# Moving the division, cutting GpSimd's splits in four, and reordering the first loads in a fused attention and expert kernel

## The chip, the core and the metric

One core of a Trainium2 chip. TensorE (PE) multiplies, VectorE (DVE) and ScalarE (ACT) do elementwise work and reductions, GpSimd (POOL) does elementwise work and issues the indirect transfers, SyncE (SP) issues the other transfers. Each engine takes its instructions in the order in which the program was written; engines wait for each other by semaphores. The metric is device time of one execution in microseconds (us).

## The reference

```python
# attention, for 4 batches x 8 heads, 768 positions, 64 dims
k_sum = k.reshape(B, H, 24, 32, D).max(axis=3)
v_sum = v.reshape(B, H, 24, 32, D).mean(axis=3)
scores_l = scale * q @ k.T, kept where |i - j| < 16
scores_s = scale * q @ k_sum.T + log(32)
a = softmax(concat(scores_l, scores_s))
x = a @ concat(v, v_sum)                    # then (4, 768, 512)
# a token's expert: argmax of 8 logits, or the expert of the token before it
fresh_e = argmax(x @ w_gate);  local = sigmoid(x @ w_local)
e = fresh_e if s == 0 or local < 0.5 else previous e
out = softmax(logits)[e] * (relu(x @ w1[e]) @ w2[e])   # 512 -> 1024 -> 512
```

All is float32. The products of the experts are made of three matmuls on split operands: each operand is a high part (the value rounded to the format fp32r) and a low part (the rest), and hi x hi, hi x lo and lo x hi are added.

## The kernel before

**Attention.** A pair is two heads of one batch; there are 16 pairs, and each is worked in two groups of three blocks of 128 queries, 32 groups G in all. A group passes through stages that are issued in different rounds of one loop over G: its scores (`s_mm`, L251 mask and L257), its maximum on DVE (L264) and exponentials on ACT (L268), two rounds later its transposes on PE (L278) with copies on ACT (L279), three rounds later the second products (`a_mm`, L289) into a PSUM pool `a` of one bank, and the division `a_norm` on DVE (L300, L302, L304), which reads that bank. Before the change `a_norm` of a group stands one round after its `a_mm`, between the transposes and the maximum of that round, and two calls `small(1)` stand between its three instructions.

**Keys and values of a pair.** `load_k`, `load_q`, `load_v`, `load_w` fetch keys (two buffers), queries (three), values for the sums (two) and values for the windows (`vw`, three) through SP's queue. POOL copies the keys into overlapping windows (`windows`, L216), halves the values for their sums (`fold_v`, L209), writes the summary columns (`summaries`, L219) and spreads the value sums into `vw` (`spread_v`, L228). DVE reduces keys (L200) and values (`reduce_v`, L204); `sum_v` transposes the sums on PE (L223) and copies them on ACT. In an even round 2n POOL gets `windows(n + 1)` and `fold_v(n + 1)`, in the odd one `summaries(n + 1)` and `spread_v(n)`. A transfer into a buffer that is still to be read waits in SP's queue, and so do all transfers behind it.

**Routing.** When a batch's x is done, `x_tile` makes its logits on PE, and `route`, `early`, `second`, `gate_p`, `finish` work out each token's expert and place, in many small DVE instructions with PE steps between them. They are generators that yield the kind of the next step. Inside the attention `small(n, pe)` issues up to n of them at fixed places, from at most two chains in turn; a step LONG counts 4; a PE step is taken only where `pe` is set and at least `AGE` = 2 calls after the step before it. A round has five calls before the change (1, 1, 3, then 2 and 4 with PE), 11 in sum. After the attention `flow` places them by a plan of time: a DVE step counts `C_DVE` and its result `C_LAT` more, a PE step is issued when the plan's time has reached its operand. The first rows of tokens for the experts' fourth pair of slots are listed by matmuls at L852, the weights of the rows by L938; `self.A` holds a one-hot row of 128 for each token (L581), which L700, L727, L852 and L938 use.

**Experts.** Rows come in slots of 128, two to a pair. The first three pairs hold the most frequent experts and run while `route` and `finish` still work on the last batch. A pair is 96 matmuls of the first layer (L1015 to L1017), ReLU (L1021 ACT, L1023 DVE), and 24 of the second for each half (L988 to L990). Rows are fetched (L960) and written (L1001) by indirect transfers from POOL. A new expert's weights are split in eight chunks of 1024 columns by `split`: ACT rounds (L951), DVE or POOL subtracts (L954), by a letter for each chunk (`WBY`, `SPLIT_BY`).

Of the kernel before, what the change touches and what calls it, by code (L numbers as in the profile page):

```python
# [9 lines left out]
F32 = mybir.dt.float32  # L10
# [3 lines left out]
AF = mybir.ActivationFunctionType  # L14
ALU = mybir.AluOpType
# [4 lines left out]
P = 128  # L20
# [36 lines left out]
AGE = 2  # L57
C_T, C_PE, C_WAIT, C_LONG, C_DVE, C_LAT, AHEAD = 0.65, 0.8, 0.3, 0.9, 0.17, 0.05, 1.5

# [3 lines left out]
class Kernel:  # L63
    def __init__(self, ctx, tc, qT, kT, vT, vW, maskc, identc, wgc, w1, w2, c32c, cb16c, out):
        self.tc, self.nc, self.out = tc, tc.nc, out
        self.steps, self.credit, self.have_p, self.last, self.early_in = [], 0, 0, None, {}
        self.calls = 0
        self.t, self.q = 0.0, 0.0
        self.qT, self.kT, self.vT, self.vW = qT, kT, vT, vW
        self.w = (w1, w2)  # L70
# [73 lines left out]
    def attention(self, tick, last):  # L144
        nc, tc, ident = self.nc, self.tc, self.ident
        with ExitStack() as ctx:
# [44 lines left out]
            nc.sync.dma_start(out=t, in_=src)  # L191
            for load, n in ((load_k, 1), (load_q, 1), (load_v, 0), (load_w, 0), (load_v, 1), (load_w, 1), (load_q, 2)):
                load(n)
# [18 lines left out]
            def windows(n, eng=nc.gpsimd, t0=0, t1=NW):  # L212

                src = kp[n % 2][:, 64 * t0:64 * t0 + 1]
                win = bass.AP(src.tensor, src.offset, [src.ap[0], (64, t1 - t0), (1, WL)])
                eng.tensor_scalar(out=kb[n % 2][:, t0:t1, 0:WL], in0=win, scalar1=0.125, scalar2=1.0, op0=ALU.mult, op1=ALU.mult)  # L216

# [74 lines left out]
            def a_norm(G):  # L292
                n, g = groups[G]
                b, p = pairs[n]
                ap = live.pop(G)
                if p == 0:
                    self.xs[b, g] = wk.tile([P, NG, H * D], F32, name="xs", bufs=4)
                x = self.xs[b, g]
                dn = wk.tile([P, NG, 2, 1], F32, name="dn")
                nc.vector.tensor_scalar(out=dn, in0=ap[:, :, :, D:D + 1], scalar1=1e-9, scalar2=None, op0=ALU.add)  # L300
                self.small(1)
                nc.vector.reciprocal(out=dn, in_=dn)  # L302
                self.small(1)
                nc.vector.tensor_tensor(  # L304
                    out=x[:, :, 2 * D * p:2 * D * (p + 1)].rearrange("p u (h d) -> p u h d", h=2),
                    in0=ap[:, :, :, 0:D], in1=dn.to_broadcast([P, NG, 2, D]), op=ALU.mult)
                if p == NP - 1:
                    t = b * NU + NG * g
                    nc.sync.dma_start(out=self.x_dram[:, t:t + NG, :], in_=x)

            reduce_k(0)
            windows(0, nc.vector, 0, NW // 2)
            windows(0, nc.gpsimd, NW // 2, NW)
            summaries(0, nc.vector)
            windows(1)
            load_k(2)
            LT, LA = 2, 3
            last_g = len(groups)
            for G in range(last_g + LA):
# [7 lines left out]
                tick(G, 2)  # L327
                if G < last_g and G % GP == 0 and G:
                    sum_v(G // GP, self.spare[:, 1, 0:P])
                tick(G, 4)  # L330
                if LT <= G < last_g + LT:
                    t_stage(G - LT)
                if LA + 1 <= G <= last_g:
                    a_norm(G - LA - 1)
                tick(G, 3)
                if G < last_g:
                    s_exp(G)
                    self.small(3)
                if G == 0:
# [3 lines left out]
                if G < last_g:  # L343
                    self.small(2, True)
                if LA <= G:
                    a_mm(G - LA)
                if G < last_g:
                    n, g = groups[G]
# [14 lines left out]
                    else:  # L363
                        if n == 0:
                            sum_v(0, self.bank("t")[:, 0:P])
                            reduce_v(1)
                        elif n + 1 < N:
                            summaries(n + 1)
                            reduce_v(n + 1, folded.pop(n + 1))
                        spread_v(n)  # L370
                        if n + 3 < N:
                            load_k(n + 3)
                            load_q(n + 3)
                else:
                    a_norm(G - LA)
                tick(G, 1)
# [12 lines left out]
    def wait(self):  # L389
        while len(self.steps) > 1:  # L390
            yield "WAIT"

# [91 lines left out]
    def route(self, b):  # L484
# [55 lines left out]
        yield "DVE"  # L540
        v.tensor_tensor_scan(out=s2, data0=c["keep"], data1=o2, initial=0.0, op0=ALU.mult, op1=ALU.add)
        yield "PE"
        m = self.bank("t")
# [29 lines left out]
        if b == 1:  # L573
# [3 lines left out]
                                   op0=ALU.mult, op1=ALU.max)  # L577
        for u in range(NU):
            if u % 2 == 0:
                yield "DVE"  # L580
            v.tensor_scalar(out=self.A[:, b * NU + u, :], in0=c["iota128"], scalar1=lanf[:, u:u + 1],  # L581
                            scalar2=None, op0=ALU.is_equal)

# [20 lines left out]
    def second(self):  # L604
# [14 lines left out]
        yield "DVE"  # L619
        v.scalar_tensor_tensor(out=cnt, in0=self.er, scalar=2.0 * P, in1=cnt, op0=ALU.mult, op1=ALU.max)  # L620
        yield "DVE"
        v.tensor_tensor(out=self.lbe[:, 0:1], in0=e1f, in1=self.e0f, op=ALU.is_equal)
# [14 lines left out]
        yield "DVE"  # L637
        v.tensor_scalar(out=self.adj[:, 2], in0=self.is1, scalar1=-2.0, scalar2=7.0, op0=ALU.mult, op1=ALU.add)

    def gate_p(self, b0, b1):  # L640
# [30 lines left out]
        for i in range(3):  # L671
            yield "DVE"
            v.tensor_copy(out=p3[:, :, i, 0], in_=r)
            if i < 2:
                yield "DVE"
                v.tensor_tensor(out=r, in0=r, in1=p3[:, :, i, 0], op=ALU.subtract)

    def early(self, j, ef=None, places=None):

        nc, wk, c = self.nc, self.rw, self.c  # L680
        v = nc.vector
        n = self.early_b(j) * NU
        ef, places = ef or self.e0f, places or (2.0 * j, 2.0 * j + 1)
        in0 = self.early_in[j] = wk.tile([P, n, 2, 1], BF16, name=f"ein{j}")
# [19 lines left out]
        for i in range(2):  # L704
            yield "DVE"
            v.scalar_tensor_tensor(out=self.lb[:, 0:n], in0=in0[:, :, i], scalar=64.0, in1=self.lb[:, 0:n], op0=ALU.mult, op1=ALU.add)

    def early_b(self, j):
# [3 lines left out]
    def early_p(self, b0, b1, *pairs):  # L712
        nc, wk, v = self.nc, self.rw, self.nc.vector
        yield from self.gate_p(b0, b1)
        for j in pairs:
            while j not in self.early_in:
                yield "WAIT"
            in0 = self.early_in[j]
            n = self.early_b(j) * NU
# [31 lines left out]
    def finish(self):  # L751
# [4 lines left out]
        npi = wk.tile([P, E], I32, name="npi")  # L756
        nci = wk.tile([P, E], I32, name="nci")
        q = wk.tile([P, E], F32, name="q")
        yield "DVE"
# [164 lines left out]
        yield from rows(FIRST, SLOTS)  # L924
        yield from self.gate_p(B - 1, B)
        n = SLOTS - EARLY
        eq = wk.tile([P, NT, n], F32, name="eqp")
# [21 lines left out]
    def split(self, which, c0, c1, src, eng):  # L949
        hi, lo = self.hi[which][:, c0:c1], self.lo[which][:, c0:c1]  # L950
        self.nc.scalar.copy(out=hi, in_=src)  # L951
        if eng is self.nc.vector:
            self.dve(1.1)
        eng.tensor_tensor(out=lo, in0=src, in1=hi.bitcast(F32), op=ALU.subtract)  # L954

# [388 lines left out]
```

## Time and profile before

| | us |
|---|---|
| times of three runs | 493.34, 495.4, 497.38 (median 495.4) |
| the profiled execution | 497.38 |
| its span, first to last instruction | 495.6 |
| PE busy | 448.0 (90% of the span) |
| DVE, ACT, POOL busy | 285.2, 216.4, 190.1 |
| mean granted clock of PE | 0.957 |

A row of the order of time gives start, length, engine, line, operation, what is written from what, the shape and the count; in brackets the idle time before it and the instruction that ended it. A row of groups gives busy time, mean length in ns, and idle time with its releasers. A `q` behind an engine's name is its sequencer, where transfers are issued.

### The profile page before, as it was taken

Reading aid. Unit: us, or ns where it says so; the run is one execution under the profiler, and the core shown is the slowest. Engines: PE = TensorE matmul, PEld = TensorE weight load, DVE = VectorE, ACT = ScalarE, POOL = GpSimd, SP = SyncE. Lnnn points to the kernel's source line nnn. Section 1 sums busy time; section 2 is a strip of 40 time slices with the busy share of each in tenths; the row PEclk is TensorE's granted clock in tenths of the full one; section 3 lists DMA queues with packets and bytes.
Section 4 is the critical chain, followed back from the end, with each engine's and each line's share of the span. In section 5 each row is a group of like instructions: output and inputs, shape, how many; then the busy total and the mean of one; then the engine's idle time right before and its main releaser. Section 6 shows DMA issues by size and latency. Waiting matters only on the chain. (4 is left out here: it accounts for less than half of the span.)

```text
span 495.6 us, 11918 instructions
## 1 busy us (share of the span) xinstructions
PE 448.0 (90%) x4400; PEld 389.0 (78%) x4400; DVE 285.2 (58%) x623; ACT 216.4 (44%) x478; POOL 190.1 (38%) x152
## 2 busy tenths in 40 slices
PE   6899988878779999889899999999999999999990
PEld 5687776767567789688799998989879898977980
DVE  4686698777663756965522223158686226777610
ACT  3698876677535322702110201054556116274500
POOL 2685553373401230631102111146477204566720
PEclk9799999979879999979999999999999999999996
DMA  8999799678212084016402010119498503847840
GB/s 317 404 370 375 285 321 395 239 256 341 88 56 75 1 296 173 21 65 231 197 1 85 23 65 28 58 43 323 145 324 280 197 33 110 309 165 253 291 162 26
DMA packets 23622, 92.04 MB, mean 186 GB/s; under 512 B 2927, under 2 KB 3567, under 8 KB 19440
## 3 DMA queue, kind: packets, MB, share of 16 engines
q1 hardware_dynamic: 18752, 76.11, 42.2%
q0 software_dynamic: 4640, 14.68, 8.7%
q8 instruction: 41, 0.67, 0.5%
q14 instruction: 45, 0.37, 0.2%
q10 hardware_dynamic: 144, 0.20, 0.1%
HBM read 78.40 MB, written 13.11 MB: 185 GB/s over the span
## 5 line engine op out<-in xcount | busy, mean ns | idle before, releaser
L1015 PE MATMUL bs<-xT,h 128*128 128x256 f32 x384 | 110.6, 288 | 0.0
L1016 PE MATMUL bs<-xT,h 128*128 128x256 f32 x384 | 109.5, 285 | 0.5 <-DVE xT L966 0.5
L1017 PE MATMUL bs<-xT,l 128*128 128x256 f32 x384 | 109.6, 285 | 0.1
L1021 ACT ACTIVATE hT<-bs 128x512 fp32r<-128x512 f32 x48 | 28.7, 598 | 131.8 <-PE bs L1017 127.7
L960 POOL DMA_INDIRECT xg<-x_dram,gidx x32 | 34.8, 1089 | 127.5 <-POOLq L1191 57.7
L988 PE MATMUL ba<-h,hT 128*128 128x512 f32 x192 | 77.7, 405 | 0.4
L1023 DVE SCALAR_TENSOR_TENSOR hT<-bs,hT 128x512 fp32r<-128x512 f32 x48 | 33.0, 690 | 77.7 <-ACT hT L1021 66.8
L1016 PEld LDWEIGHTS bs<-xT,h 128*128 128x128 f32 x384 | 74.5, 194 | 1.1 <-DVE xT L966 0.7
L990 PE MATMUL ba<-h,hT 128*128 128x512 f32 x192 | 75.1, 391 | 0.0
L989 PE MATMUL ba<-l,hT 128*128 128x512 f32 x192 | 75.0, 391 | 0.0
L1015 PEld LDWEIGHTS bs<-xT,h 128*128 128x128 f32 x384 | 74.5, 194 | 0.7 <-issue 0.2
L1017 PEld LDWEIGHTS bs<-xT,l 128*128 128x128 f32 x384 | 74.4, 194 | 0.5 <-DVE l L954 0.5
L954 DVE TENSOR_TENSOR l<-stg,h 128x1024 fp32r<-128x1024 f32 x35 | 67.9, 1949 | 11.3 <-ACT h L951 8.1
L268 ACT ACTIVATE pr<-bs,nm 128x120 f32<-128x120 f32 x192 | 52.0, 372 | 25.2 <-DVE nm L264 24.8
L951 ACT CAST h<-stg 128x1024 fp32r<-128x1024 f32 x56 | 57.2, 1052 | 11.3 <-PE ba L990 8.2
L954 POOL TENSOR_TENSOR l<-stg,h 128x1024 fp32r<-128x1024 f32 x21 | 51.4, 2467 | 20.4 <-ACT h L951 20.4
L1001 POOL DMA_INDIRECT out_dram<-yo,sidx x26 | 31.1, 1197 | 59.1 <-DVE yo L1000 40.2
L988 PEld LDWEIGHTS ba<-h,hT 128*128 128x128 f32 x192 | 36.1, 188 | 8.0 <-ACTq L1191 0.6
L289 PE MATMUL ba<-vw,pt 120*64 120x65 f32 x768 | 33.0, 241 | 10.3 <-DVE xs L304 5.9
L990 PEld LDWEIGHTS ba<-h,hT 128*128 128x128 f32 x192 | 36.0, 188 | 7.8
L289 PEld LDWEIGHTS ba<-vw,pt 120*64 120x64 f32 x768 | 28.9, 153 | 15.7 <-issue 11.6
L989 PEld LDWEIGHTS ba<-l,hT 128*128 128x128 f32 x192 | 36.2, 189 | 6.2
(236 smaller groups left out, 672.3 us busy)
## 6 DMA issues: line engine op xcount, KB each, us to landing
stg<-in_w SPq DMA_DIRECT2D x32, 1024.0 KB, 5.7
vw<-in_vW SPq DMA_DIRECT2D x16, 780.0 KB, 4.5
kp<-in_kT SPq DMA_DIRECT2D x16, 384.0 KB, 6.3
q<-in_qT SPq DMA_DIRECT2D x16, 384.0 KB, 6.7
vt<-in_vT SPq DMA_DIRECT2D x16, 384.0 KB, 7.3
x_dram<-xs SPq DMA_DIRECT2D x8, 768.0 KB, 9.9
wst<-in_w SPq DMA_DIRECT2D x8, 512.0 KB, 8.4
xg<-x_dram,gidx POOLq DMA_INDIRECT x32, 8.4
```

The costliest lines, as they stand in the source:

```text
L268: nc.scalar.activation(out=pr[:, h, u, :], in_=sp[:, h, u, :], func=AF.Exp, bias=nm[:, h, u:u + 1], scale=1.0)
L289: nc.tensor.matmul(out=ap[64 * c:64 * c + 64, u, h, :], lhsT=pt[:, h, u, 64 * c:64 * c + 64], rhs=vw[n % 3][0:W, 2 * (NG * g + u) + c, h, ...
L951: self.nc.scalar.copy(out=hi, in_=src)
L954: eng.tensor_tensor(out=lo, in0=src, in1=hi.bitcast(F32), op=ALU.subtract)
L960: self.nc.gpsimd.indirect_dma_start(out=t, out_offset=None, in_=rows, in_offset=bass.IndirectOffsetOnAxis(ap=self.gidx[:, i:i + 1], axis=0))
L988: nc.tensor.matmul(out=ps, lhsT=ah, rhs=wh, start=first, stop=False)
L989: nc.tensor.matmul(out=ps, lhsT=ah, rhs=wl, start=False, stop=False)
L990: nc.tensor.matmul(out=ps, lhsT=al, rhs=wh, start=False, stop=last)
L1015: nc.tensor.matmul(out=ps[:, j], lhsT=wh, rhs=xh, start=(k == 0), stop=False)
L1016: nc.tensor.matmul(out=ps[:, j], lhsT=wh, rhs=xl, start=False, stop=False)
L1017: nc.tensor.matmul(out=ps[:, j], lhsT=wl, rhs=xh, start=False, stop=(k == KT - 1))
L1023: nc.vector.scalar_tensor_tensor(out=l, in0=ps, scalar=0.0, in1=h.bitcast(F32), op0=ALU.max, op1=ALU.subtract)
```

## The change

- `a_norm(G - 3)` is issued right behind `a_mm(G - 3)`, without the two `small(1)`. A round has three calls of `small` (3, 2, 4), 9 in sum, and PE steps are allowed in all of them.
- `reduce_v(n + 1)` moves ahead of `a_mm` in odd rounds.
- `sum_v` and `spread_v` of pairs 0 and 1 move behind the transposes of rounds 2 and 4; `reduce_v(1)` moves from round 1 to round 3.
- The first loads: values 0 ahead of queries 1; values 1, `vw` 1 and queries 2 behind keys 2. Half of the first `windows` is done by ACT instead of DVE.
- `split`: where POOL subtracts, four instructions of 256 columns stand for one of 1024.
- `route`: the six one-hot rows L581 become one `tensor_tensor` for all, a LONG step.
- `until(names)` lets a chain yield WAIT until another has reached a named point (`done`); it issues nothing.
- `C_DVE` is 0.1 for 0.17.

```diff
-C_T, C_PE, C_WAIT, C_LONG, C_DVE, C_LAT, AHEAD = 0.65, 0.8, 0.3, 0.9, 0.17, 0.05, 1.5
+C_T, C_PE, C_WAIT, C_LONG, C_DVE, C_LAT, AHEAD = 0.65, 0.8, 0.3, 0.9, 0.1, 0.05, 1.5
...
-            for load, n in ((load_k, 1), (load_q, 1), (load_v, 0), (load_w, 0), (load_v, 1), (load_w, 1), (load_q, 2)):
+            for load, n in ((load_k, 1), (load_v, 0), (load_q, 1), (load_w, 0)):
                 load(n)
...
-                eng.tensor_scalar(out=kb[n % 2][:, t0:t1, 0:WL], in0=win, scalar1=0.125, scalar2=1.0, op0=ALU.mult, op1=ALU.mult)
+                if eng is nc.scalar:
+                    eng.activation(out=kb[n % 2][:, t0:t1, 0:WL], in_=win, func=AF.Copy, scale=0.125)
+                else:
+                    eng.tensor_scalar(out=kb[n % 2][:, t0:t1, 0:WL], in0=win, scalar1=0.125, scalar2=1.0, op0=ALU.mult, op1=ALU.mult)
...
                 nc.vector.tensor_scalar(out=dn, in0=ap[:, :, :, D:D + 1], scalar1=1e-9, scalar2=None, op0=ALU.add)
-                self.small(1)
                 nc.vector.reciprocal(out=dn, in_=dn)
-                self.small(1)
...
-            windows(0, nc.vector, 0, NW // 2)
+            windows(0, nc.scalar, 0, NW // 2)
             windows(0, nc.gpsimd, NW // 2, NW)
             summaries(0, nc.vector)
             windows(1)
-            load_k(2)
+            for load, n in ((load_k, 2), (load_q, 2), (load_v, 1), (load_w, 1)):
+                load(n)
...
-                if G < last_g and G % GP == 0 and G:
+                if GP < G < last_g and G % GP == 0:
                     sum_v(G // GP, self.spare[:, 1, 0:P])
                 tick(G, 4)
                 if LT <= G < last_g + LT:
                     t_stage(G - LT)
-                if LA + 1 <= G <= last_g:
-                    a_norm(G - LA - 1)
+                if G in (2, 4):
+                    sum_v(G // 2 - 1, self.bank("t")[:, 0:P])
+                    spread_v(G // 2 - 1)
                 tick(G, 3)
                 if G < last_g:
                     s_exp(G)
-                    self.small(3)
+                    self.small(3, True)
...
+                n, g = divmod(G, GP)
+                if g == 1 and 0 < n < len(pairs) - 1:
+                    reduce_v(n + 1, folded.pop(n + 1))
                 if LA <= G:
                     a_mm(G - LA)
+                    a_norm(G - LA)
...
-                        if n == 0:
-                            sum_v(0, self.bank("t")[:, 0:P])
+                        if n + 1 < N and n:
+                            summaries(n + 1)
+                        if n == 1:
                             reduce_v(1)
-                        elif n + 1 < N:
-                            summaries(n + 1)
-                            reduce_v(n + 1, folded.pop(n + 1))
-                        spread_v(n)
+                        if n > 1:
+                            spread_v(n)
...
+    def until(self, *names):
+
+        while not self.done.issuperset(names):
             yield "WAIT"
...
-        for u in range(NU):
-            if u % 2 == 0:
-                yield "DVE"
-            v.tensor_scalar(out=self.A[:, b * NU + u, :], in0=c["iota128"], scalar1=lanf[:, u:u + 1],
-                            scalar2=None, op0=ALU.is_equal)
+        if b < B - 2:
+            self.done.add(("counts", b + 1))
+        yield "LONG"
+        v.tensor_tensor(out=self.A[:, ts, :], in0=c["iota128"].unsqueeze(1).to_broadcast([P, NU, P]),
+                        in1=lanf.unsqueeze(2).to_broadcast([P, NU, P]), op=ALU.is_equal)
...
         if eng is self.nc.vector:
             self.dve(1.1)
-        eng.tensor_tensor(out=lo, in0=src, in1=hi.bitcast(F32), op=ALU.subtract)
+            eng.tensor_tensor(out=lo, in0=src, in1=hi.bitcast(F32), op=ALU.subtract)
+            return
+
+        for o in range(0, c1 - c0, 256):
+            p = slice(o, o + 256)
+            eng.tensor_tensor(out=lo[:, p], in0=src[:, p], in1=hi[:, p].bitcast(F32), op=ALU.subtract)
```

More of the change, by code (lines that the diff above doesn't have):

```diff
@@ L68, in __init__ @@
         self.t, self.q = 0.0, 0.0
+        self.done = {("counts", 0), ("early", -1)}
         self.qT, self.kT, self.vT, self.vW = qT, kT, vT, vW
@@ L373, in attention @@
                             load_q(n + 3)
-                else:
-                    a_norm(G - LA)
                 tick(G, 1)
@@ L390, in wait @@
         while len(self.steps) > 1:
+            yield "WAIT"
+    def until(self, *names):
+        while not self.done.issuperset(names):
             yield "WAIT"
@@ L541, in route @@
         v.tensor_tensor_scan(out=s2, data0=c["keep"], data1=o2, initial=0.0, op0=ALU.mult, op1=ALU.add)
+        yield from self.until(("counts", b))
         yield "PE"
@@ L620, in second @@
         v.scalar_tensor_tensor(out=cnt, in0=self.er, scalar=2.0 * P, in1=cnt, op0=ALU.mult, op1=ALU.max)
+        self.done.add(("counts", B - 1))
         yield "DVE"
@@ L638, in second @@
         v.tensor_scalar(out=self.adj[:, 2], in0=self.is1, scalar1=-2.0, scalar2=7.0, op0=ALU.mult, op1=ALU.add)
+        self.done.add("second")
     def gate_p(self, b0, b1):
@@ L676, in gate_p @@
                 v.tensor_tensor(out=r, in0=r, in1=p3[:, :, i, 0], op=ALU.subtract)
+        self.done.add(("weights", b0))
     def early(self, j, ef=None, places=None):
@@ L682, in early @@
         n = self.early_b(j) * NU
+        yield from self.until(("early", j - 1))
         ef, places = ef or self.e0f, places or (2.0 * j, 2.0 * j + 1)
@@ L706, in early @@
             v.scalar_tensor_tensor(out=self.lb[:, 0:n], in0=in0[:, :, i], scalar=64.0, in1=self.lb[:, 0:n], op0=ALU.mult, op1=ALU.add)
+        self.done.add(("early", j))
     def early_b(self, j):
@@ L717, in early_p @@
                 yield "WAIT"
+            yield from self.until(("weights", 0))
             in0 = self.early_in[j]
@@ L757, in finish @@
         nci = wk.tile([P, E], I32, name="nci")
+        yield from self.until("second", ("early", EARLY // 2 - 1))
         q = wk.tile([P, E], F32, name="q")
@@ L925, in finish @@
         yield from self.gate_p(B - 1, B)
+        yield from self.until(("weights", 0), ("weights", 2))
         n = SLOTS - EARLY
```

## The prediction

> **What bounds the kernel now.** I read the span first, then busy time and granted clock in stretches of 20 us, then the waits and the order of time in each stretch where TensorE (PE) is not full.
>
> ```profile
> span 495.6 us, 11918 instructions
> ```
> ```profile
> 0.00:20.00 20.00, 13.94 (x194) 11.74 (x194) 8.91 (x16) 9.06 (x29) 6.36 (x14) 0.83 0.93 349
> 20.00:40.00 20.00, 19.69 (x429) 16.36 (x425) 17.55 (x38) 18.51 (x63) 16.38 (x18) 1.00 1.01 381
> 80.00:100.00 20.00, 16.04 (x300) 12.73 (x290) 16.36 (x44) 12.52 (x43) 8.19 (x8) 0.91 0.80 299
> 100.00:120.00 20.00, 16.49 (x270) 13.77 (x272) 14.68 (x35) 14.75 (x43) 11.56 (x9) 0.83 0.81 290
> 120.00:140.00 20.00, 13.41 (x229) 10.44 (x221) 15.27 (x60) 11.15 (x36) 7.56 (x7) 0.90 0.34 117
> 200.00:220.00 20.00, 15.21 (x100) 13.45 (x99) 17.02 (x37) 9.06 (x11) 12.25 (x7) 0.83 0.15 53
> 240.00:260.00 20.00, 17.53 (x144) 16.40 (x143) 6.51 (x9) 3.67 (x6) 2.00 (x2) 1.00 0.08 31
> ```
>
> The columns are busy time of PE, its weight load, VectorE (DVE), ScalarE (ACT), GpSimd (POOL), then the granted clock, the DMA share and GB/s. PE's work sets the end, and what can be won is PE's idle time and the clock it loses. From 80 to 140 us PE is idle for 60 - 45.94 = 14.1 us, and the clock loses 0.09, 0.17 and 0.10 of 20 us, 7.2 us together. From 200 to 220 it is idle 4.8 us. In the first 20 us it is idle 6.1 us, but there the transfers are full (share 0.93, then 1.01).
>
> **The start.** The columns of the next rows are start, length, engine, line, and in brackets idle time and its releaser.
>
> ```profile
> 0.73 0.39 SPq L162 DMA_DIRECT2D kp<-in_kT  x1
> ...
> 4.83 0.95 DVE L200 TENSOR_REDUCE ks<-kp 128x24 f32<-128x768 f32 x1 [3.81 <-DMA kp<-in_kT]
> ...
> 14.16 0.39 PE L223 MATMUL bs<-ident,va 128*24 128x128 f32 x1 [2.64 <-DVE va L204]
> ...
> 16.09 0.33 SPq L167 DMA_DIRECT2D vt<-in_vT  x1
> ...
> 19.06 1.02 POOL L209 TENSOR_TENSOR vf<-vt 128x384 f32<-128x384 f32 x1 [0.72 <-DMA vt<-in_vT]
> ...
> 20.11 0.55 DVE L204 TENSOR_REDUCE va<-vf 128x24 f32<-128x384 f32 x1 [1.31 <-POOL vf L209]
> ...
> 20.53 0.62 PEld L257 LDWEIGHTS bs<-kb,q 64*64 64x64 f32 x24 [0.28 <-POOL kb L219]
> ...
> 25.73 0.35 PE L251 MATMUL bs<-me 64*64 64x360 bf16 x4
> ```
>
> The change takes the wait at 14.16 away: the sums of the first two pairs move behind the transposes of groups 2 and 4. It loads the third keys before the second values, and hands half of the first windows to ACT. But group 4's scores need `summaries(2)`, which stands on POOL behind `fold_v(2)`, and that waits for the third values. Before them lie the same bytes as now, so they land at 19 us again and group 4 starts at 20.5 again. PE is now merely idle later: from about 16 to 20.5 in one piece, with the half clock behind it where the groups follow each other closely. Two things are new. `reduce_v(2)` stands in DVE's order ahead of the division of group 0 and of `reduce_v(1)`; it ends at 20.66 (20.11 + 0.55), the division takes about 0.9 (L304 below and two small ones), `reduce_v(1)` 0.95, so the second values' buffer is free at 22.5. SyncE's load of the fourth values, issued at 16.09 now, waits for that buffer, and behind it in SP's queue wait the third `vw` and the fifth keys and queries. A load with an empty queue takes some 4 us (the first keys, asked for at 0.73, are there at 4.83), then fold 1.0 and summaries 0.4: the scores of group 6 start at 28.0 and not at 25.73. The half clock over groups 4 and 5 costs about the same, at the same time. I take **+2.3**; bounds 0 (the sums' two waits gone are enough) and +5 (a load takes its median 7.3, below).
>
> ```profile
> vt<-in_vT SPq DMA_DIRECT2D x16, 384.0 KB, 7.3
> ```
>
> **The attention groups that carry routing.** The single bank of the second products (L289) is freed by the division (L300, L302, L304). Now the division is queued a group later, with routing steps between its instructions.
>
> ```profile
> 84.21 0.56 DVE L304 TENSOR_TENSOR xs<-ba,dn 128x384 f32<-128x384 f32 x1
> ...
> 84.87 1.57 PE L289 MATMUL ba<-vw,pt 120*64 120x65 f32 x24 [2.25 <-issue]
> ```
> ```profile
> 101.09 2.35 POOL L954 TENSOR_TENSOR l<-wst,h 128x1024 fp32r<-128x1024 f32 x1 [4.59 <-ACT h L951]
> ...
> 103.41 0.44 POOL L219 TENSOR_SCALAR kb<-ks 128x288 f32<-128x288 f32 x1
> 103.90 0.85 PE L257 MATMUL bs<-kb,q 64*64 64x120 f32 x24 [1.97 <-POOL kb L219]
> ...
> 107.48 1.57 PE L289 MATMUL ba<-vw,pt 120*64 120x65 f32 x24 [1.33 <-DVE xs L304]
> ```
> ```profile
> 124.61 0.45 PE L700 MATMUL bt<-ebt,A 128*128 128x4 bf16 x12 [1.87 <-DVE ebt L696]
> ...
> 132.47 0.92 PE L289 MATMUL ba<-vw,pt 120*64 120x65 f32 x24 [1.24 <-DVE xs L304]
> ...
> 137.78 0.92 PE L289 MATMUL ba<-vw,pt 120*64 120x65 f32 x24 [2.46 <-DVE xs L304]
> ```
>
> With the division right behind its products the bank is free a whole group before it is wanted again, whatever DVE does in between. That removes 2.25 + 1.33 + 1.24 + 2.46 = 7.28 us of idle. The wait at 124.61 comes from the one-hot rows:
>
> ```profile
> L581 DVE TENSOR_SCALAR A<-c,lanf 128x128 bf16<-128x128 f32 x24 | 11.7, 543 | 0.0
> L843 DVE TENSOR_TENSOR eq<-c,blk 128x768 f32<-128x768 f32 x1 | 0.9, 934 | 0.0
> L954 POOL TENSOR_TENSOR l<-stg,h 128x1024 fp32r<-128x1024 f32 x21 | 51.4, 2467 | 20.4 <-ACT h L951 20.4
> L209 POOL TENSOR_TENSOR vf<-vt 128x384 f32<-128x384 f32 x14 | 14.2, 1011 | 8.1 <-DMA vt<-in_vT 4.5 <-DVE va L204 2.4 <-DVE cnt L553 1.2
> ```
>
> Six of 543 ns, 3.3 us, become one of the size of L843, 0.93. I count the 1.87 as gone; sum 9.2. Of the 7.2 us of clock I take half, 3.6, since the wait at 103.90 stays: it is POOL's order (`summaries` behind a weight split). There the quarters cost: two rows give (2467 - 1011) / 640 = 2.3 ns an element and so 0.72 us for 256, four of them 2.9 and not 2.47, **+0.4** once; later splits have POOL's idle time as cover (2.0 of 20 us busy from 240 on), and cost 0.4 on each of 21 chunks if it were gone. Attention: **-12.8**, bounds -5 (the bank's waits, partly replaced) and -19 (12 idle, 7.2 clock).
>
> What is late next there: DVE, with 46.3 of 60 us busy. Waiting in order for the products costs it little, because the maximum (L264) of the next group must wait for the scores that PE issues after those products. Fewer steps a group (9 for 11) and PE steps allowed at three calls in three delay the chain by less than a group. The `until` names issue nothing; they are a guard only.
>
> [...]
>
> **The end of routing.** PE stands before the matmuls that list the first rows.
>
> ```profile
> 201.13 2.04 DVE L823 TENSOR_SCALAR o<-pt 128x24 int32<-128x24 int32 x1
> ```
> ```profile
> 206.77 5.65 POOL L954 TENSOR_TENSOR l<-stg,h 128x1024 fp32r<-128x1024 f32 x2 [1.56 <-ACT h L951]
> ```
> ```profile
> 207.83 2.34 DVE L835 CAST_PREDICATED blk<-e,pt 128x24 f32<-128x24 int32 x1
> 210.20 2.33 DVE L843 TENSOR_TENSOR eq<-c,blk 128x96 f32<-128x96 f32 x1
> ```
> ```profile
> 213.09 0.80 PE L852 MATMUL bt<-bt,A 128*128 128x8 bf16 x24 [4.79 <-DVE bt L848]
> ```
> ```profile
> 218.74 0.60 ACT L1021 ACTIVATE hT<-bs 128x512 fp32r<-128x512 f32 x1 [8.76 <-PE bs L1017]
> 221.62 0.60 ACT L1021 ACTIVATE hT<-bs 128x512 fp32r<-128x512 f32 x1 [2.28 <-PE bs L1017]
> ```
> ```profile
> 236.46 0.17 DVE L659 TENSOR_SCALAR sm<-sm 128x6 f32<-128x6 f32 x1
> 236.67 0.19 DVE L661 RECIPROCAL sm<-sm 128x6 f32<-128x6 f32 x1
> ```
> ```profile
> 242.83 1.34 PE L938 MATMUL bt<-bp,A 128*128 128x108 bf16 x24 [2.47 <-DVE bp L934]
> ```
>
> Three small DVE instructions took 6.7 us together; small ones take about 0.2 (L659), so some 6.0 of it is standing until a POOL split ends. L835 ended and L843 began between the two splits of 206.77: DVE gets in at the border of two POOL instructions. With quarters a border comes every 0.72, half of it on average, 1.1 for three: DVE's chain is 4.9 shorter. Against this stands the planner: a dependent step now counts 0.10 + 0.05 and takes 0.21 (236.46 to 236.67), where it counted 0.17 + 0.05. Some 34 steps lie between the start of `finish` and L852, so PE's matmuls are placed 2.0 us too early. The wait becomes 4.79 - 4.9 + 2.0 = 1.9, a gain of 2.9. The slow clock behind it (first block of the pair from L852's end, 213.9, to 218.74, 4.8 against 2.9) cost 1.9; half goes, 1.0. The denser plan should bring L938 inside the third pair and remove its 2.47; with the same doubt I take half, 1.2. Together **-5.1**, bounds 0 and -9.2.
>
> **Sum.** The profiled execution took 497.4 us (span 495.6 and 1.8 around it), 2.0 above the median 495.4. 497.4 + 2.3 + 0.4 - 12.8 - 5.1 = 482.2; on the median **480.2**.
>
> **Rivals.**
> 1. DVE and the transfers take PE's place. For it: DVE is busy 17.55 of 20 us from 20 to 40 and 46.3 of 60 later, and the loads are full to 40. Then only about half of the 12.8 comes and half of the 5.1: 480.2 + 6.4 + 2.6 = 489.2. Against: after 80 us the transfer share is 0.8 and less.
> 2. The quarters don't let DVE in, because POOL's next one starts at once: nothing at the end of routing, 485.3. Against: the border at 210.2.
> 3. The other side: in every group the division, now ahead of the next maximum, delays the exponentials. ACT is busy 18.51 of 20 us from 20 to 40, so ACT would be the bound; price up to 0.9 (L304 0.56 and two small ones near 0.2, as L659) in 28 groups, 25 us, so 505. It decides from about 0.6 us a group. Against: the next maximum waits for the next scores anyway, and their 0.85 (L257) covers the division.
> 4. Short gaps keep the clock: removing them wins their idle time alone, 480.2 + 3.6 + 1.0 = 484.8. [...]
>
> **Chances.** Forecast 0.58, its own range 470 to 489; rival 1 0.17, rival 2 0.09, rival 3 0.10, rival 4 0.06. The range goes from 469 to 494, which leaves out rival 3 and some tails. About 1% (5 us) is what a measurement can tell from no change. Faster (under 490.4): 0.55 + 0.09 + 0.08 + 0.06 = 0.78; slower (over 500.4): rival 3's upper part, 0.08 with tails; the same: 0.14.
>
> **What would show it.** Right: no L289 that waits for L304 between 80 and 140; L257 still waiting some 2 us behind a POOL split near group 26; L823, L835 and L843 under 1 us; L852's wait between 0 and 3. At the start: the load of the fourth values after 21 us and group 6 later than 25.73. Wrong: exponentials that wait for the maximum in every group, PE waits at L512 to L938 that add up to more than 7.3, or a clock under 0.9 from 80 to 140 without long gaps.

## The result, and the profile after

The changed kernel takes 480.2 us (479.85 to 480.55) beside 496.1 for the kernel before (four runs by now), a ratio of 0.968 with a 95% interval of 0.963 to 0.974. One of its four runs took 708.2 us at a mean granted clock of 0.56; it counts in the median of 480.2, which would be 479.85 without it, and not in the range or the ratio. The forecast was 480.2. The profiled execution of it took 479.85 us, 17.5 less than the one of before, and its span of 478.1 falls short of the old 495.6 by as much. The medians lie 15.9 apart: the profiled execution of before was the slowest of its four, so what is read off the two profiles is good to some 1.6 us.

The first thing to do with such a result is to cut the span where both kernels do the same thing. The first matmul of the experts (L1015 before, L1039 after) divides attention from the rest. From the order of time of TensorE (PE), before and then after; columns as in the prediction:

```profile
147.46 0.39 PE L1015 MATMUL bs<-xT,h 128*128 128x256 f32 x1
```
```profile
139.13 0.38 PE L1039 MATMUL bs<-xT,h 128*128 128x256 f32 x1
```

So 8.3 us were won ahead of it and 9.2 behind it (495.6 - 147.46 = 348.1, 478.1 - 139.13 = 339.0). The prediction's sum had -10.1 (start, quarters and attention) and -5.1. The stretches of 20 us of the changed kernel, with the columns of before:

```profile
0.00:20.00 20.00, 12.55 (x197) 10.59 (x197) 7.78 (x14) 10.10 (x32) 5.92 (x14) 0.91 0.89 327
20.00:40.00 20.00, 18.53 (x380) 15.33 (x381) 16.09 (x35) 14.69 (x50) 14.06 (x15) 0.91 0.93 343
80.00:100.00 20.00, 17.62 (x347) 13.93 (x340) 16.91 (x48) 14.76 (x50) 9.63 (x9) 1.00 1.01 380
100.00:120.00 20.00, 16.86 (x310) 13.21 (x310) 16.43 (x41) 16.47 (x49) 14.43 (x16) 1.00 0.85 315
120.00:140.00 20.00, 17.28 (x270) 14.16 (x268) 16.58 (x61) 12.42 (x37) 6.39 (x6) 0.83 0.34 118
200.00:220.00 20.00, 18.80 (x170) 17.51 (x169) 17.17 (x33) 5.67 (x9) 10.81 (x11) 1.00 0.70 249
```

PE is idle 8.2 us from 80 to 140 where it was idle 14.1, and loses 0.17 of 20 us of clock, 3.4, where it lost 7.2. From 200 to 220 the idle time fell from 4.8 to 1.2. The start lost: 7.5 + 1.5 idle us in the first 40 for 6.1 + 0.3. In the list of waits of PE (sum, times, longest) the two waits at the end of routing are now

```profile
PE bt L870 <- DVE bt L866: 0.7, 1, 0.7
PE bt L957 <- DVE bp L953: 0.5, 1, 0.5
```

for 4.79 at L852 and 2.47 at L938, the same lines before. The groups of weight splits on the page, GpSimd (POOL) and VectorE (DVE); the third row is DVE's before:

```profile
L978 POOL TENSOR_TENSOR l<-stg,h 128x256 fp32r<-128x256 f32 x84 | 73.9, 915 | 2.3 <-ACT h L970 1.6
L973 DVE TENSOR_TENSOR l<-stg,h 128x1024 fp32r<-128x1024 f32 x35 | 46.5, 1338 | 16.2 <-ACT h L970 13.1
```
```profile
L954 DVE TENSOR_TENSOR l<-stg,h 128x1024 fp32r<-128x1024 f32 x35 | 67.9, 1949 | 11.3 <-ACT h L951 8.1
```

A chunk costs POOL 3.66 us now and not 2.47, and DVE's own splits, untouched by the change, 1.34 and not 1.95. The wait behind a split near group 26 is there, in POOL's and PE's order of time:

```profile
101.32 2.78 POOL L978 TENSOR_TENSOR l<-wst,h 128x256 fp32r<-128x256 f32 x4 [4.18 <-ACT h L970]
104.06 0.43 POOL L223 TENSOR_SCALAR kb<-ks 128x288 f32<-128x288 f32 x1
...
104.55 0.85 PE L261 MATMUL bs<-kb,q 64*64 64x120 f32 x24 [2.38 <-POOL kb L223]
```

The signs of being right that the prediction had named are as it said, but one: the load of the fourth values, at 20.48 and not after 21. Of the signs of being wrong one is there in part: the clock is 0.83 from 120 to 140, behind a gap of only 1.23 us, though 0.94 over the whole stretch from 80 to 140. That looked like a forecast right for its reasons. The experiments say otherwise.

### The profile page after: what moved, and what is told of

Its sections match the earlier page's. It is cut to its first block, busy times and chain, and to the rows that moved or that the text cites. A ratio compares the mean times of both kernels' runs of the same rounds, so it can differ in the third digit from the quotient of the medians.

```text
span 478.1 us, 11984 instructions
## 1 busy us (share of the span) xinstructions
PE 441.2 (92%) x4400; PEld 383.0 (80%) x4400; DVE 256.9 (54%) x602; ACT 216.3 (45%) x479; POOL 214.8 (45%) x227
## 5 line engine op out<-in xcount | busy, mean ns | idle before, releaser
L1039 PE MATMUL bs<-xT,h 128*128 128x256 f32 x384 | 109.9, 286 | 0.0
L984 POOL DMA_INDIRECT xg<-x_dram,gidx x32 | 37.1, 1160 | 124.8 <-POOLq L1215 54.2
L978 POOL TENSOR_TENSOR l<-stg,h 128x256 fp32r<-128x256 f32 x84 | 73.9, 915 | 2.3 <-ACT h L970 1.6
L1040 PEld LDWEIGHTS bs<-xT,h 128*128 128x128 f32 x384 | 73.5, 192 | 1.3 <-DVE xT L990 0.8
L1039 PEld LDWEIGHTS bs<-xT,h 128*128 128x128 f32 x384 | 73.5, 191 | 0.7 <-issue 0.2
L970 ACT CAST h<-stg 128x1024 fp32r<-128x1024 f32 x56 | 57.2, 1053 | 11.9 <-PE ba L1014 10.9
L272 ACT ACTIVATE pr<-bs,nm 128x120 f32<-128x120 f32 x192 | 51.9, 371 | 14.0 <-DVE nm L268 10.5
L973 DVE TENSOR_TENSOR l<-stg,h 128x1024 fp32r<-128x1024 f32 x35 | 46.5, 1338 | 16.2 <-ACT h L970 13.1
L1025 POOL DMA_INDIRECT out_dram<-yo,sidx x26 | 28.2, 1085 | 46.7 <-DVE yo L1024 21.3
L261 PE MATMUL bs<-kb,q 64*64 64x120 f32 x768 | 27.2, 276 | 8.3 <-POOL kb L223 7.6
L268 DVE TENSOR_REDUCE nm<-bs 128x6 f32<-128x720 f32 x32 | 28.7, 898 | 5.9 <-ACT l L481 2.7
```

The lines of the kernel that those rows point to most:

```text
L272: nc.scalar.activation(out=pr[:, h, u, :], in_=sp[:, h, u, :], func=AF.Exp, bias=nm[:, h, u:u + 1], scale=1.0)
L978: eng.tensor_tensor(out=lo[:, p], in0=src[:, p], in1=hi[:, p].bitcast(F32), op=ALU.subtract)
L984: self.nc.gpsimd.indirect_dma_start(out=t, out_offset=None, in_=rows, in_offset=bass.IndirectOffsetOnAxis(ap=self.gidx[:, i:i + 1], axis=0))
L1039: nc.tensor.matmul(out=ps[:, j], lhsT=wh, rhs=xh, start=(k == 0), stop=False)
L1040: nc.tensor.matmul(out=ps[:, j], lhsT=wh, rhs=xl, start=False, stop=False)
```

## Experiments

"Changed" is the changed kernel (480.2), "before" the kernel before (496.1 to 496.8 beside these runs). Times are medians of four to ten runs. "Theory 1" and so on are those of the expectation that stands above the result.

### The division late again

```diff
+                if LA + 1 <= G <= last_g:
+                    a_norm(G - LA - 1)
                 if G in (2, 4):
...
                     a_mm(G - LA)
-                    a_norm(G - LA)
...
+                else:
+                    a_norm(G - LA)
                 tick(G, 1)
```

> The changed kernel (480.2 us), but the division of a round's second products is again queued a round later, behind the transposes of the next round; the two routing steps between its instructions do not come back. Theory 1 (the prediction's largest term): the place of the division in VectorE's order is what made TensorE wait for the bank, so L293 waits for the division again between 80 and 140 us, some 7.3 us of idle and about 3.6 us of clock: 491 us, clock under 1.00 in 80 to 120. Theory 2: it was the routing steps between its instructions and the 11 steps a round that delayed it; without them the place alone costs under 3 us: 481 to 483, and no wait of L293 over 1 us.

480.4 us, and the first expert matmul at 139.2 as in the changed kernel. Yet the bank's waits are back. From the waits of PE between 78 and 139 us, this kernel and then the changed one:

```profile
PE ba L293 <- DVE xs L306: 4.0, 3, 2.1
```
```profile
PE bt L522 <- DVE val L519: 1.4, 1, 1.4
PE bt L715 <- DVE ebt L711: 1.2, 1, 1.2
PE bs L227 <- DVE va L205: 0.9, 1, 0.9
PE bt L555 <- DVE sc L551: 0.5, 1, 0.5
```

PE waits for DVE either way, 4.0 us in sum; only the instruction that stands first in line is another. Neither theory had this: the waits do come back (against theory 2), and they cost nothing (against theory 1). It fits that DVE, busy 49.9 of the 60 us from 80 to 140 in the changed kernel, is behind as a whole; no run tests that by itself.

### Each of three other parts undone

```diff
-C_T, C_PE, C_WAIT, C_LONG, C_DVE, C_LAT, AHEAD = 0.65, 0.8, 0.3, 0.9, 0.1, 0.05, 1.5
+C_T, C_PE, C_WAIT, C_LONG, C_DVE, C_LAT, AHEAD = 0.65, 0.8, 0.3, 0.9, 0.17, 0.05, 1.5
```

> The changed kernel, but the plan after the attention counts a VectorE step at 0.17 us again and not at 0.10. Theory 1 (the prediction): the lower price places TensorE's steps 2 us too early, so with 0.17 the waits of L870 (0.7) and L957 (0.5) go and nothing else changes: 478 to 480. Theory 2: the lower price packs the steps closer, and that, not the quarters, brought the listing of the rows from 65.6 us behind the first expert matmul to 47.5 and so ahead of the weight splits; with 0.17 the listing comes later, into the splits at 193 to 208, and L870 waits 2 to 4 us: 482 to 485.

493.4 us: 13.2 of the gain are gone. PE's order of time shows where:

```profile
239.78 2.34 PE L957 MATMUL bt<-bp,A 128*128 128x108 bf16 x24 [7.44 <-DVE bp L953]
```

The last early pair had ended at 232.3. From there eighteen DVE steps (L766 to L953), fourteen small ones and four of about 1 us, ran one behind the other with no expert matmul left beside them. The plan is worked in calls, one for each piece of expert work; its last 14 calls here have no such piece and are called bare below. Theory 2 had the direction but not the place or the size: the listing (L870) waits 2.9, the weights of the rows (L957) 7.4, and the granted clock falls with both: 0.83 from 200 to 220 us, where the first listing starts (207.3), 0.93 from 220 to 240 and 0.90 from 240 to 260.

```diff
-        for o in range(0, c1 - c0, 256):
-            p = slice(o, o + 256)
-            eng.tensor_tensor(out=lo[:, p], in0=src[:, p], in1=hi[:, p].bitcast(F32), op=ALU.subtract)
+        eng.tensor_tensor(out=lo, in0=src, in1=hi.bitcast(F32), op=ALU.subtract)
```

> The changed kernel, but GpSimd's weight splits are whole again (one of 1024 columns, 2.47 us, for four of 915 ns). Theory 1 (the prediction): VectorE's short steps at the end of routing (L841, L853, L861: 0.18, 0.19 and 0.26 us now) get in at the borders of the quarters, so they stand for 2 us each again and L870's wait goes from 0.7 to 4 or 5: 480.2 + 2.9 + 1.0 + 1.2 - 0.4 = 484.9. Theory 2: they are short now because the plan issues them at 183 to 185 us, where GpSimd splits nothing (its splits of that pair stand at 193 to 208); whole splits change nothing there, and 3.66 us a chunk become 2.47, which wins at most the 1.2 us of one chunk at the wait near group 26 (2.38): 479 to 480.5.

486.7 us, 6.5 more. The first expert matmul is at 138.9, so all of it lies behind the attention. The chain at 183 to 185 us is as short as with quarters, as theory 2 said. But the second list of rows, 20 us later, meets the splits. DVE's and POOL's order of time of this kernel:

```profile
198.94 3.63 DVE L973 TENSOR_TENSOR l<-stg,h 128x1024 fp32r<-128x1024 f32 x1
...
203.68 3.02 DVE L866 TENSOR_TENSOR bt<-eq,c 128x768 bf16<-128x768 f32 x1
```
```profile
199.06 2.42 POOL L973 TENSOR_TENSOR l<-stg,h 128x1024 fp32r<-128x1024 f32 x1
...
202.68 3.21 POOL L973 TENSOR_TENSOR l<-stg,h 128x1024 fp32r<-128x1024 f32 x1 [1.21 <-ACT h L970]
```

A DVE split that takes 1.21 alone took 3.63 and ended 1.09 behind POOL's 2.42, L866 (0.95 alone) took 3.02 and ended 0.81 behind POOL's 3.21, and L870 waits 3.7. So theory 1's mechanism holds, at another place than the prediction's. Beside it L1007 waits 2.1 us for a rounded weight, which it doesn't with quarters.

```diff
-        yield "LONG"
-        v.tensor_tensor(out=self.A[:, ts, :], in0=c["iota128"].unsqueeze(1).to_broadcast([P, NU, P]),
-                        in1=lanf.unsqueeze(2).to_broadcast([P, NU, P]), op=ALU.is_equal)
+        for u in range(NU):
+            if u % 2 == 0:
+                yield "DVE"
+            v.tensor_scalar(out=self.A[:, b * NU + u, :], in0=c["iota128"], scalar1=lanf[:, u:u + 1],
+                            scalar2=None, op0=ALU.is_equal)
```

> The changed kernel (480.2 us) with the one-hot rows as six instructions again. Theory 1 (the prediction): only the wait before the early listing comes back, 0.7 us more than now (1.87 for 1.2): 480.9. Theory 2 (VectorE's backlog sets the pace from 80 to 140): each batch's six instructions stand for 3.3 us and longer beside GpSimd (4 of them took 2.28, two 1.28), so three batches in the attention cost 2.4 us each, part of it hidden: 483 to 486, with L293 waiting for the division again near 83 us.

490.3 us, 10.1 more, and more than either theory gave. The first expert matmul comes at 145.3, 6.2 later. In the attention four of the rows (L594 here) took

```profile
120.54 3.11 DVE L594 TENSOR_SCALAR A<-c,lanf 128x128 bf16<-128x128 f32 x4
```

against 0.95 to 0.99 for all six (L592) in the changed kernel. The half clock lasted about 14 us between 104 and 136 in this execution, and 7 in that of the changed kernel, so up to some 3 of the 6.2 are clock. The other 4 us are at the second list of rows, in an unexpected way:

```profile
206.66 7.39 DVE L868 TENSOR_TENSOR bt<-eq,c 128x768 bf16<-128x768 f32 x2
...
207.72 5.51 POOL L980 TENSOR_TENSOR l<-stg,h 128x256 fp32r<-128x256 f32 x8
...
214.11 1.34 PE L872 MATMUL bt<-bt,A 128*128 128x64 bf16 x24 [4.96 <-DVE bt L868]
```

Here eight quarters ran through in 5.51 us, 0.69 each, and DVE's second instruction got in only behind the last. In the changed kernel the same meeting went the other way. POOL's eight quarters, and DVE's rows among them:

```profile
200.78 8.06 POOL L978 TENSOR_TENSOR l<-stg,h 128x256 fp32r<-128x256 f32 x8
```
```profile
200.98 1.38 DVE L866 TENSOR_TENSOR bt<-eq,c 128x768 bf16<-128x768 f32 x1
...
202.28 1.76 DVE L973 TENSOR_TENSOR l<-stg,h 128x1024 fp32r<-128x1024 f32 x1
...
203.97 1.49 DVE L866 TENSOR_TENSOR bt<-eq,c 128x768 bf16<-128x768 f32 x1
```

PE's wait behind that list is 0.7 us in all eight traces in which these splits meet the second list at this place, the changed kernel's two among them; it is 5.0 in this one alone. So a border between two POOL instructions was a chance to get in, and no more. What decides it isn't settled.

### Parts alone, in the kernel before

```diff
-C_T, C_PE, C_WAIT, C_LONG, C_DVE, C_LAT, AHEAD = 0.65, 0.8, 0.3, 0.9, 0.17, 0.05, 1.5
+C_T, C_PE, C_WAIT, C_LONG, C_DVE, C_LAT, AHEAD = 0.65, 0.8, 0.3, 0.9, 0.1, 0.05, 1.5
```

> The kernel before (496.1 us) with one number changed: the plan counts a VectorE step at 0.10 us. Three early pairs give 100 calls of the plan as cover. By the plan's own arithmetic the routing after the attention takes 111 calls in the kernel before (10 of them behind the last early pair, with no expert matmul beside them), 115 in the changed kernel with 0.17 (14 bare), 98 here and 87 in the changed kernel (none bare). Theory 1 (the bare calls): the wait at L938 (2.47) and the clock lost behind it go, L852's 4.8 gets smaller since the listing comes 10 calls earlier: 486 to 490. Theory 2 (the prediction's): the plan only places TensorE's steps too early, L852 waits longer: 496 to 498.

496.2 us, no change (0.999, 0.997 to 1.002). The bare calls and the wait at L938 are gone as theory 1 said, but another wait has come. From DVE's and POOL's order of time, and the waits of PE:

```profile
207.99 5.36 DVE L874 TENSOR_SCALAR fl<-fl,c 128x8 f32<-128x8 f32 x1
```
```profile
208.58 4.74 POOL L954 TENSOR_TENSOR l<-stg,h 128x1024 fp32r<-128x1024 f32 x2
```
```profile
PE bt L917 <- DVE tot L911: 5.8, 1, 5.8
```

An instruction on 8 columns stands through two whole splits. The time is theory 2's, but not its wait: L852 isn't in the list of waits any more. The closer plan brings a later part of the chain right into the splits, and alone it wins nothing.

```diff
-                self.small(1)
                 nc.vector.reciprocal(out=dn, in_=dn)
-                self.small(1)
...
-                if LA + 1 <= G <= last_g:
-                    a_norm(G - LA - 1)
...
-                    self.small(3)
+                    self.small(3, True)
...
                     a_mm(G - LA)
+                    a_norm(G - LA)
...
-                else:
-                    a_norm(G - LA)
```

> The kernel before (496.1 us) with the division right behind its products, without routing steps between its instructions, and TensorE steps allowed in all three calls of a round; nothing else. Theory 1 (the prediction): the bank's waits of 7.28 us go and 3.6 us of clock with them: 485. Theory 2 (from the changed kernel with the division late, which was no slower): VectorE's backlog sets the pace there, and the wait only moves to another TensorE instruction: 493 to 496, with waits at L512, L700 or L223 in place of those at L289.

493.1 us, 3.2 less, where the prediction's sum has 10.9 for this. No L289 waits for the division any more, but in PE's list there stands

```profile
PE bs L223 <- DVE va L204: 9.8, 8, 2.7
```

The reduction of the values is now what comes late, eight times. Theory 2 is right: the wait moves. A part of it is order again: the reduction stands behind the division here, whose three instructions take 0.9, while the change also moves `reduce_v` ahead of the products, which this kernel leaves out (in the changed kernel L227 waits 1.7 in all). The division and that move together, with no other part, weren't tried.

```diff
-C_T, C_PE, C_WAIT, C_LONG, C_DVE, C_LAT, AHEAD = 0.65, 0.8, 0.3, 0.9, 0.17, 0.05, 1.5
+C_T, C_PE, C_WAIT, C_LONG, C_DVE, C_LAT, AHEAD = 0.65, 0.8, 0.3, 0.9, 0.1, 0.05, 1.5
...
-            v.tensor_scalar(out=self.A[:, b * NU + u, :], in0=c["iota128"], scalar1=lanf[:, u:u + 1],
...
+        v.tensor_tensor(out=self.A[:, ts, :], in0=c["iota128"].unsqueeze(1).to_broadcast([P, NU, P]),
...
+        for o in range(0, c1 - c0, 256):
...
```

> The kernel before (496.1 us) with three parts of the change and no other: one-hot rows in one instruction, weight splits in quarters, a VectorE step counted at 0.10 us in the plan (87 calls of the plan, none bare, as in the changed kernel). Start, division and the order of the reductions stay as before. Undone alone in the changed kernel they cost 10.1, 6.5 and 13.2 us, together more than the whole gain of 16; the plan's number alone won nothing (496.2). Theory 1 (the prediction's sum): the attention's order, 7.3 us of idle and 3.6 of clock, is missing here, so 489 to 491. Theory 2 (the three hold each other, and the order of the division only moves waits): all of the gain but the start's loss is here: 478 to 481.

480.9 us (478.6 to 482.2), with the old start, the old division and the bank's waits:

```profile
PE ba L289 <- DVE xs L304: 4.9, 5, 2.5
```

That is in theory 2's range, and these three parts are nearly all of the gain. Undone one at a time they cost 10.1, 6.5 and 13.2, together 29.8: each is worth its price only beside the others. What is left to the division's order and the routing's calls is small: the changed kernel with the old start, below, has them and the same start as this one, and takes 478.0, 2.9 less. The two were run on different chips, and the 2.9 are near the 3.2 above. The one-hot rows alone in the kernel before weren't tried.

### The start

The start's edits undone, all other parts kept:

```diff
-            for load, n in ((load_k, 1), (load_v, 0), (load_q, 1), (load_w, 0)):
+            for load, n in ((load_k, 1), (load_q, 1), (load_v, 0), (load_w, 0), (load_v, 1), (load_w, 1), (load_q, 2)):
...
-            windows(0, nc.scalar, 0, NW // 2)
+            windows(0, nc.vector, 0, NW // 2)
...
-                if G in (2, 4):
-                    sum_v(G // 2 - 1, self.bank("t")[:, 0:P])
-                    spread_v(G // 2 - 1)
...
+                        if n == 0:
+                            sum_v(0, self.bank("t")[:, 0:P])
+                            reduce_v(1)
...
```

> The changed kernel with the start of the kernel before: its order of the first loads, the first half windows on VectorE, the sums of the first two pairs and the second pair's reduction at their old places. Theory 1 (the prediction's +2.3): the new start loses, group 6 starts at 25.7 again and not at 27.6, and what follows comes as much earlier: 477.5 to 478.5. Theory 2: the lag of the new start is taken in by waits later in the attention (groups 22 to 26 are level with the kernel before already), so the old start gives the same, 479.5 to 480.5. Theory 3: the sums' two waits (2.6 and 2.3 us) come back and the end moves later, 481 to 483.

478.0 us, 2.2 less than the changed kernel and 2.4 less than the kernel with the late division, which ran on the same chip: theory 1, and near the forecast's 2.3. What the new start loses shows in the rate of the transfers, a column for each 0.75 us from 10 to 40 us. The changed kernel:

```profile
GB/s 419 369 418 410 430 440 391 376 374 393 403 361 131 41 12 86 348 423 408 374 406 432 381 420 399 399 297 308 401 418 432 348 337 335 350 385 299 406 386 353
```

From 19 to 22 us next to nothing moves. The queue's rows around it:

```profile
20.42 0.43 POOL L223 TENSOR_SCALAR kb<-ks 128x288 f32<-128x288 f32 x1
20.48 0.33 SPq L168 DMA_DIRECT2D vt<-in_vT  x1
20.48 0.55 DVE L205 TENSOR_REDUCE va<-vf 128x24 f32<-128x384 f32 x1 [5.20 <-POOL vf L210]
...
20.90 1.11 PE L261 MATMUL bs<-kb,q 64*64 64x120 f32 x24 [4.63 <-POOL kb L223]
```

SyncE's load of the fourth values stands until a buffer of values is free, and the loads behind it in the queue stand with it. The idle 4.63 us of PE are the visible loss. That the hole in the transfers is the lasting one is the reading that the next two runs speak for.

```diff
                             windows(n + 1)
+                            reduce_k(n + 1)
+                            if n == 1:
+                                summaries(n + 1)
                             fold_v(n + 1)
-                            reduce_k(n + 1)
...
-                        if n + 1 < N and n:
+                        if n + 1 < N and n > 1:
                             summaries(n + 1)
```

> The changed kernel with one step of the start moved: the summaries of the third pair stand ahead of the fold of its values on GpSimd, so that they wait for the keys alone. Theory 1: group 4's scores start at 16.6 us and not at 20.9, the idle piece of 4.6 us and the half clock behind it go, and the lead lasts: 476 to 478. Theory 2: the transfers pace the start (share 0.89 to 0.93), so the next groups wait for third values or keys instead, and under 1 us is left: 479.5 to 480.5.

479.8 us. Group 4's scores do start at 16.5, and PE waits 3.4 us at the next instruction (L227, the third sum) instead: theory 2. The hole is still there, with 102, 25, 37 and 184 GB/s from 19 to 22 us. With the buffer freed earlier as well:

```diff
-                if GP < G < last_g and G % GP == 0:
+                if 2 * GP < G < last_g and G % GP == 0:
                     sum_v(G // GP, self.spare[:, 1, 0:P])
...
+                if G == 5:
+                    sum_v(2, self.bank("t")[:, 0:P])
...
-                if g == 1 and 0 < n < len(pairs) - 1:
+                if g == 1 and n == 1:
+                    reduce_v(1)
+                elif g == 1 and 1 < n < len(pairs) - 1:
                     reduce_v(n + 1, folded.pop(n + 1))
...
+                            if n == 2:
+                                reduce_v(2, folded.pop(2))
                             windows(n + 1)
...
-                        if n == 1:
-                            reduce_v(1)
```

> The changed kernel with the start's order mended: the summaries of pair 2 ahead of the fold of its values, the second pair's reduction in round 3 ahead of the third's, the third's in round 4, its sum behind the transposes of round 5. Theory 1: what the new start loses for good is a hole in the transfers near 20 us (22 and 65 GB/s at 20 to 22 us, where the loads wait for the second values' buffer); with the buffer free earlier the hole closes, group 6 starts before 26 us and the lead lasts: 475.5 to 478. Theory 2: something else of the start paces it (transposes of the sums, half clock), and the time stays at 479.5 to 480.5.

477.5 us (477.2 to 478.2), and the hole is closed:

```profile
GB/s 384 394 406 431 418 449 362 389 368 403 394 401 414 431 411 377 403 427 397 446 414 423 387 390 418 427 402 386 380 411 394 406 434 414 324 191 281 377 249 199
```

Group 6 starts at 22.7 where the changed kernel has 27.59. The time is theory 1's: of those 4.9 us 4.7 are left at the last group, 1.9 at the first expert matmul and 2.7 at the end. Behind the last group L293 waits 2.1 us for the division, where the changed kernel waits 1.05 for ACT. The edit closes the hole and takes the wait of L227 away at once, so the two aren't told apart; but the kernel with the old start has no hole either (237 GB/s at the least from 10 to 40 us) and takes as little time, 478.0 for 477.5.

### One wait more, and the same kernel again

```diff
-WBY = "GVGVVGVG"
+WBY = "VGGVVGVG"
```

> The kernel with the mended start (477.5 us), and the first two weight chunks change engines: chunk 0 is split by VectorE in round 24, chunk 1 by GpSimd in round 25, behind the summaries that now wait for a split. Theory 1: the wait of L261 near 100 us (2.37) goes, and with it the half clock of some 4 us that began there: 473 to 475.5. Theory 2: VectorE's backlog sets the pace there, so its 1.2 us of splitting delays the division or a reduction by as much: 476.5 to 478.

Beside it ran the changed kernel once more, with no edit:

> The changed kernel itself, unchanged, beside the mended one on the same chip. Theory 1: 479.8 to 480.6 as before, so that the mended start wins 2 to 3 us and its differences to the other kernels of this study, taken on other chips, hold. Theory 2: chips differ by as much as these variants, 477 to 479 or over 481.

The changed kernel took 481.4 us there, over 1 us more than at first, so differences of 1 to 1.5 us between kernels that weren't run together say nothing. The other took 479.7, 1.7 less than the changed kernel beside it; the mended start alone had won 2.7. The 479.7 lie above the ranges of both theories. The wait of L261 near 100 us is gone, as theory 1 said, but some 3.4 us of half clock at 102 to 106 us are still there, and a new wait stands on DVE's side:

```profile
PE bt L536 <- DVE pm L533: 3.3, 1, 3.3
```

So nothing was won: theory 2's mechanism, a wait for DVE in place of the one that went.

## Why the prediction was right, and where it was not

**The total** was right to the last digit, by luck in good part: on the profiled executions the same sum says 482.2, and 479.85 was measured. Of its terms two were right in size (the start, and what the quarters cost near group 26), one was near in size for a wrong reason (the attention, 12.8 for about 11), and one was about half the size (the end of routing, 5.1 for 9.2); these two errors partly cancelled.

**The start, +2.3.** Right in size (2.2 by the old start put back) and in kind: idle in one piece (4.63 us), a granted clock of 0.57 behind it (20.90 to 24.30 us), a late load of the fourth values. The step about the buffer was wrong: the load took the third values' buffer, freed by the fold at 20.45, not the second's at 22.5. Group 6 came at 27.59 for 28.0.

**The quarters, +0.4.** The wait near group 26 grew from 1.97 to 2.38 as said. What the quarters win stood in the term for the end of routing; undone, they cost 6.5, since DVE's splits and the second list get in between them. The estimate of 0.72 us for a quarter is near the 0.69 measured with DVE shut out; over all 84 the mean is 0.915, and 1.01 in the eight with DVE's rows among them.

**The attention, -12.8.** To the first expert matmul 8.3 us were won, with the start's 2.3 and the quarters' 0.4 lost: about -11 for the term. Its main step failed. "With the division right behind its products the bank is free", and "That removes 7.28 us of idle": the place of the division alone wins nothing (division late again, 480.4), and with its other edits, in the kernel before, it wins 3.2 (division early alone). The step took a wait for DVE as a matter of the place of one instruction; the runs showed that the next instruction in line waits for DVE instead. The one-hot rows, put at 1.87 us, were the larger part: undone, they cost 6.2 us to the first expert matmul, up to 3 of it clock. The half of the lost clock, 3.6, came out as 7.2 - 3.4 = 3.8, but see below for how little that says.

**The end of routing, -5.1.** Measured -9.2. The failed step: "PE's matmuls are placed 2.0 us too early", a price for the plan's smaller number. It counted some 34 steps up to the listing and took the wait at L852 for the whole matter. The plan places some 200 DVE steps behind the attention, and three early pairs cover just 100 of its calls; before, 10 calls ran bare, with the wait at L938 at their end. That "the denser plan should bring L938 inside the third pair" was right, but it was priced at 1.2 us: the plan's number is worth 13.2 us with the other two parts and nothing without them. That the short steps at L841 to L861 are short now (0.18 to 0.26) was forecast, yet not for the reason given: they run at 183 us, where POOL splits nothing.

**The rivals.** Rival 1 (DVE takes PE's place) fits what happened with the division, though not the sum. Rival 2 (quarters don't let DVE in) happened in one kernel, the one with six rows, where PE waits 5 us. Rival 3 is refuted: the exponentials' waits for the maximum fell from 24.8 to 10.5 us in all. Rival 4 (short gaps keep the clock) has a case for and a case against, below.

## What to carry to other kernels

A wait in the profile names the instruction that stood first in line; before counting it as won, ask whether the engine it waited for is behind as a whole, and if so relieve that engine and don't move its instructions. Where a plan issues work beside other work, count how much work the cover holds: a step's price in the plan was worth nothing here (496.2 for 496.3) or a dozen us (493.4 for 480.2), by whether the last steps still had cover. A load that waited for its buffer until 20.48 us held back those behind it in its queue, and the transfers fell from some 400 GB/s to 12; look for such holes in the rate, since idle time beside them may be won at one instruction (4.63 us at L261) and lost at the next (3.4 at L227).

## What the runs showed of the hardware

**The half clock followed a gap or didn't.** The changed kernel twice, the same wait of L261 near 104 us (2.38 and 2.37), and the stretch of 2 us behind it (the granted clock is third from the end):

```profile
106.00:108.00 2.00, 2.00 (x37) 1.91 (x35) 1.93 (x4) 1.93 (x7) 1.92 (x2) 1.00 0.98 337
```
```profile
106.00:108.00 2.00, 2.00 (x27) 1.98 (x27) 1.72 (x4) 1.84 (x7) 1.92 (x2) 0.52 0.99 309
```

In the first of them a gap of 1.23 at 123.1 was followed by some 7 us of half clock, in the second a gap of 1.31 at the same place by none. Added up over windows of 2 us, the half clock (0.50 in the windows inside a stretch) came in stretches of 3.4, 6.8 or 10.2 us, from 4 to 150 us in all these kernels and up to 440 in the changed kernel and the one before: 6.8 at 12 to 20 us and 3.4 at 84 to 90 in the one before, 10.2 at 122 to 134 with the division early alone. So the clock behind a gap cost 0, 1.7, 3.4 or 5.1 us beyond the gap itself. Not all of it reached the time: between 80 us and the first expert matmul the first execution lost 3.4 us of clock and the second 1.7, yet both reached that matmul at the same time (139.13 and 139.10). The second waited longer instead; among its waits between 78 and 140 us is one for the division, which the first doesn't have:

```profile
PE ba L293 <- DVE xs L306: 2.3, 1, 2.3
```

Gaps of 1.23 and 2.37 us were followed by half clock, gaps of 1.31 and 2.38 by none. What decides it isn't shown.

**Short instructions of POOL shared with DVE, but not evenly.** Eight quarters in a row took 5.51 us with DVE shut out and 8.06 with DVE let in, in the rows above. With DVE shut out a quarter took 0.69, four of them 2.8, little more than the 2.4 or 2.5 of a whole one.
